# A two-stage attention and gated-convolution kernel: PSUM as eight shared banks, the whole convolution on VectorE, w_in loaded in four parts, q loaded first, and a new written order

## The chip, the core and the metric

The kernel runs on one core of one Trainium2 chip. A core has a matrix engine (TensorE, "PE" in the profile, with its weight loads "PEld" shown apart), a vector engine (VectorE, "DVE"), a scalar engine (ScalarE, "ACT"), GpSimd ("POOL") and a queue engine (SyncE, "SP"). Each engine takes its own instructions in order; semaphores order them between engines. Matmul results go to PSUM, which has eight banks; everything else lives in SBUF, and DMA queues move data between SBUF and the chip's main memory. The metric is the device time of one execution in microseconds, lower being better.

## What is computed

There are 8 batches, 8 heads, 576 positions and a head width of 64. The first stage is an attention without softmax, whose rows are normalised; the second is a gated feed-forward block with a three-tap convolution along the sequence. Inputs and output are float32.

```python
kv  = einsum('bhsd,bhse->bhde', k, v)
out = einsum('bhsd,bhde->bhse', q, kv)
rms = sqrt(mean(out * out, axis=-1, keepdims=True) + 1e-06)
x   = (out / rms * g_norm)             # then (B, S, H * D) = (8, 576, 512)
h   = maximum(x @ w_in, 0.0)           # w_in (512, 1024)
conv_out = sum over k in 0..2 of conv_w[k] * (h shifted along the sequence by k - 1, zeros outside)
gate = 1.0 / (1.0 + exp(-conv_out))
result = h * gate @ w_out              # w_out (1024, 512)
```

## The kernel before

The program is written as some forty small operations, and a long string, ORDER, lists every call of them in the order in which they are issued. Each engine keeps that order: a loop at the end ties every instruction to the one before it on its engine. A token such as `hm.0.6@2` calls `hm(0, 6)` and gives it buffer 2 of its ring; `:1` picks the other of two engines; tokens like `unread.6@0` carry a count. So the order is fixed by hand or by a search beforehand, and there is no scheduler at run time.

**Loads.** `pre` (L207) starts the first loads: k and v of heads 0 and 1 as float32 on SP's queue, the convolution weights and the gain vector (into `cw_rows`) on ACT's queue, and the rest of batch 0 in ten pieces of two heads on POOL's queue (L230), which converts to bf16 on the way. In between, DVE clears constants and POOL makes the identity. `Lq`, `Lk`, `Lv` (L290) load the other batches, batch 1 in two halves; each of q, k and v has two buffers in SBUF, so a load waits until the batch before last has been read. `Li` (L304) loads w_in in two halves of 512 columns and `Lo` (L311) w_out in two halves, all on POOL's queue. `ca` (L317) casts the float32 pieces on DVE; `ct`, `pg`, `pc` transpose the convolution weights and prepare scaled taps; `pl` (L263) sets the selection matrix `sel` on POOL.

**Attention, for a pair of heads t of a batch b.** `kv` (L344) multiplies k and v, twelve small matmuls for each pair; `kvc` (L330 on ACT, L332 on DVE) copies the two halves into a block-diagonal `kvbd`. `qt0` and `qt` (L366) transpose q on PE, and `qc0` and `qc` copy it to `qT`. `ot` (L405, L406) forms the output in PSUM, `sq` squares it on ACT, `oc` copies it to SBUF. Batch 0 is normalised directly, pair by pair: `on` (PE, a matmul with `ones`), `nl` (ACT, reciprocal root, L440), `mu0` (DVE, L455). The other batches are normalised in groups: `ss` (PE, L469) collects sums of squares with `sel`, `ln` (ACT) takes the reciprocal root, `sl` (four DVE instructions) splits it into bf16 parts, `sp` (PE, L499) spreads them again, and `mu` (DVE, L505) multiplies. The result is x of that batch.

**Feed-forward.** `hm(b, f)` (L517) makes block f of 128 columns of h for one batch: eight matmuls of 288 columns. `re` (L526, L528) applies the ReLU out of PSUM. The convolution of two blocks j runs on DVE: `ta` (L540, L541) scales the two outer taps, `aa` (L547) and `ab` (L553) add them up; `sg` (L582) is the sigmoid on ACT and `mg` (L588) the product with h on DVE. For batch 0, blocks 0 to 3 take another way: `dg` (L558) makes twelve diagonal matrices `dgw` on ACT at the start, `cm` (L568) does the three taps as matmuls on PE, and `sg` (L579) reads the sum from PSUM. Batches 0, 1, 6 and 7 go through the convolution alone, 2 and 3 together and 4 and 5 together. `om(p, m, f0)` (L598) multiplies 128 rows of a pair p of batches with w_out, eight matmuls of 512 columns, for pairs 0 and 3 in two halves of four; `ea` (L330) copies the row block out on ACT into one of eight row buffers, and `st` (L609) stores it (256 KB) from SP's queue.

**PSUM.** `ring` (L158) gives three buffers of two banks (`a0` to `a2`: q transposes, `ot`, `on`, `sp`, `hm`, `cm`, fills) and two of one bank (`b0`, `b1`: `kv`, `ss`, `om`). A buffer is free when the last reader of its former tile has done.

**Fills.** `unread.n` (L402) issues n matmuls on constants whose result nobody reads; the order places ten such groups.

ACT's tables: `act_table` (L200) loads one of two sets, one for the reciprocal root and one for the sigmoid, whenever the wanted set differs from the last.

Of the kernel before, what the change touches and what calls it, by code (L numbers as in the profile page):

```python
# [51 lines left out]
FP32 = mybir.dt.float32  # L52
# [24 lines left out]
ot.2.1@0 cm.0.1@1 sq.2.1@0 oc.2.1@0 qc.2.1@0 sg.0.1 hm.1.0@2 ot.2.2@0 hm.1.1@1 re.1.0 ot.2.3@2 sq.2.2@1 oc.2.2@1
re.1.1 sq.2.3@2 kv.3.0.4@1 oc.2.3@2 mg.0.1 hm.1.3@0 ta.1.2@0 mg.0.0 Lo.0 ta.1.0@1 kvc.3.0.4.0@1 hm.1.4@1 re.1.3
qt.3.1@2 Lo.1 Lq.4.0@0 Lv.4.0@0 ta.1.1 aa.1.0 kvc.3.0.4.1 ot.2.0@0 re.1.4 ab.1.0 sq.2.0@3 ta.1.3 qc.3.1@1 oc.2.0@3
qt.3.0@1 ot.3.3@2 ss.2@0 sq.3.3@4 qc.3.0@2 ot.3.2@0 sq.3.2@5 Lk.4.0@0 oc.3.3:1@7 ot.3.0@1 oc.3.2:1@6 om.0.0.0@1  # L80
ot.3.1@2 sq.3.0@6 aa.1.1 sq.3.1@7 hm.1.7@0 ss.3 oc.3.0:1@4 Lv.5.0@1 om.0.0.4 hm.1.5@1 ln.1@0 oc.3.1@5 re.1.7
hm.1.6@2 Lk.5.0@1 re.1.5 ab.1.1 sl.1@0 sp.2.1@0,1 al.x2@1 al.x1@0 om.0.3.0@0 ea.0.0@0 re.1.6 mu.2.2 sp.3.0@2,0
mu.2.3 sg.1.1 sg.1.3 mu.3.1 sg.1.2 mu.3.0 om.0.2.0@1 unread.1@1 sp.2.0@1,0 mu.2.1 mu.2.0 om.0.3.4 ea.0.3@1 sg.1.0
qt.4.0@2 qt.4.1@0 qc.4.1:1@3 hm.2.5@1 kv.4.0.4@0 re.2.5 kvc.4.0.4.0@0 qc.4.0@0 mg.1.0 kvc.4.0.4.1 sp.3.1@2,0 mg.1.1
Lq.5.0@1 ta.1.6@1 mu.3.2 om.0.2.4 ot.4.3@1 mu.3.3 hm.2.6@2 ea.0.2@2 sq.4.3@0 oc.4.3@1 ta.1.7 re.2.6 hm.3.7@0
Lv.6.0@0 Lk.6.0@0 ta.1.4@0 aa.1.3 ta.1.5 re.3.7 ot.4.0@1 ab.1.3 hm.2.4@2 sq.4.0@1 oc.4.0@2 Lq.7.0@0 kv.5.0.4@0
ot.4.2@0 hm.3.4@1 aa.1.2 sg.1.6 sg.1.7 kvc.5.0.4.0:1@1 om.0.1.0@1 re.2.4:1 qt.5.0@2 sq.4.2@2 oc.4.2@5 re.3.4 ab.1.2
kvc.5.0.4.1:1 ot.4.1@0 sg.1.5 hm.3.5@1 sq.4.1@3 oc.4.1@4 mg.1.3 qc.5.0@4 qt.5.1@2 ta.2.4@1 ot.5.0@0 om.0.1.4 re.3.5
# [571 lines left out]
```

## Time and profile before

| | before |
|---|---|
| median of 3 runs | 192.92 us (191.09 to 193.53) |
| the profiled execution | 192.61 us |
| its span, first to last instruction | 190.8 us |
| mean granted TensorE clock | 0.980 |
| ACT table loads | 8, 1283 ns each |
| fills (L402) | 27 in the order |
| last PE work ends, about | 186.84 us |

Times inside a profile are microseconds from the start of the span. The page gives, for each engine, its busy time, its share of the span and its number of instructions. The row PEclk cuts the span into 40 slices of 4.77 us and gives the granted TensorE clock in tenths of full speed; 9 stands for 90% or more. "PEld" is the loading of weights, which overlaps matmuls. The chain of waits follows the work that ended last back from the end, one piece per line: start, length, engine, tile, line, and how many instructions. A row by stage gives the length of the stage, then busy time and number of instructions of the engines, the granted clock, and the load of the DMA engines. Durations of matmuls are modelled and include their way through the array, so the spacing of many in a row is the better measure of what one costs.

Some rows used below, in microseconds for one: ACT `re` 0.653, `sq` 0.656, `oc` 0.661, `ea` 0.597, `nl` 0.740, `sg` 0.767 for one batch and 1.254 for two, `kvc` 0.216 (one pair of heads) to 0.378 (four); DVE `mu` 0.810, a tap of `ta` 0.38, `aa`, `ab` and `mg` 0.75 for one batch and 1.35 for two, `oc` 0.752, `qc` 0.756.

Early landings, each as issue plus time to landing: q of the four head pairs of batch 0 at 6.1, 8.4, 10.6 and 12.9 us; w_in's halves at 20.3 and 27.2; k, the last of batch 2's but q, at 33.6, and q of batch 2 at 36.5.

### The profile page before, as it was taken

Reading aid. Unit: us, or ns where it says so; the run is one execution under the profiler, and the core shown is the slowest. Engines: PE = TensorE matmul, PEld = TensorE weight load, DVE = VectorE, ACT = ScalarE, POOL = GpSimd, SP = SyncE. Lnnn points to the kernel's source line nnn. Section 1 sums busy time; section 2 is a strip of 40 time slices with the busy share of each in tenths; the row PEclk is TensorE's granted clock in tenths of the full one; section 3 lists DMA queues with packets and bytes.
Section 4 is the critical chain, followed back from the end, with each engine's and each line's share of the span. In section 5 each row is a group of like instructions: output and inputs, shape, how many; then the busy total and the mean of one; then the engine's idle time right before and its main releaser. Section 6 shows DMA issues by size and latency. Waiting matters only on the chain.

```text
span 190.8 us, 4315 instructions
## 1 busy us (share of the span) xinstructions
PE 177.8 (93%) x1782; PEld 105.8 (55%) x1804; DVE 144.2 (76%) x253; ACT 155.5 (81%) x256; POOL 29.0 (15%) x52
## 2 busy tenths in 40 slices
PE   5876899999999999999999999999999999999991
PEld 1334475677654676766554775455467665544440
DVE  5734158757898999988899979999999999971000
ACT  2787678899999899999999999997589989765341
POOL 7986007004400040500000000000000000000000
PEclk9996699999999999999999999999999999999999
DMA  6999999999999989995005321000510005413675
GB/s 150 196 197 204 203 204 205 203 205 206 204 204 204 168 109 204 156 200 87 0 3 195 118 77 57 0 0 3 202 73 0 3 0 220 174 46 141 226 268 193
DMA packets 26363, 26.27 MB, mean 138 GB/s; under 512 B 1232, under 2 KB 21736, under 8 KB 26344
## 3 DMA queue, kind: packets, MB, share of 16 engines
q0 software_dynamic: 20704, 15.96, 54.5%
q1 hardware_dynamic: 5600, 10.03, 14.5%
q8 instruction: 14, 0.23, 0.4%
q14 instruction: 5, 0.04, 0.1%
q10 hardware_dynamic: 40, 0.01, 0.0%
HBM read 32.52 MB, written 9.44 MB: 220 GB/s over the span
## 4 chain that ended last, share of the span: by engine, by line
PE 85%; ACT 8%; DMA 2%; issue 1%; DVE 1%; ACTq 0%
PE h_ps L517 34%; PE om_ps L598 33%; PE qt_ps L366 4%; PE kv_ps L344 4%; PE sp_ps L499 3%; PE o_ps L406 2%; ACT dgw L558 2%; DMA cw_rows<-in_g_norm_dram 2%; PE ss_ps L469 1%; ACT sq L419 1%; ACT kvbd L330 1%; PE unread_ps L402 1%; PE o_ps L405 1%; ACT taps L579 1%; PE cp_ps L568 1%
## 5 line engine op out<-in xcount | busy, mean ns | idle before, releaser
L517 PE MATMUL h_ps<-xT,w_in_sb 128*128 128x288 bf16 x512 | 68.0, 286 | 0.7 <-ACT h L526 0.4
L598 PE MATMUL om_ps<-w_out_sb,h 128*128 128x512 bf16 x276 | 65.8, 379 | 0.9 <-issue 0.3
L517 PEld LDWEIGHTS <-w_in_sb 128*128 128x128 bf16 x512 | 49.2, 98 | 17.1 <-issue 2.4
L598 PEld LDWEIGHTS <-h 128*128 128x128 bf16 x288 | 26.9, 98 | 31.7 <-issue 3.3
L526 ACT ACTIVATE h<-h_ps 128x576 bf16<-128x576 f32 x62 | 39.1, 653 | 3.3 <-PE h_ps L517 3.1
L582 ACT ACTIVATE taps<-taps,cwn 128x576 bf16<-128x576 bf16 (+1 forms) x44 | 39.9, 944 | 0.4 <-DVE taps L553 0.2
L330 ACT ACTIVATE row<-om_ps 128x512 f32<-128x512 f32 x36 | 21.5, 597 | 16.7 <-PE om_ps L598 15.8
L588 DVE TENSOR_TENSOR h<-h,taps 128x1152 bf16<-128x1152 bf16 (+1 forms) x24 | 22.8, 953 | 5.0 <-ACT taps L582 4.9
L505 DVE SCALAR_TENSOR_TENSOR xT<-o,cw,sp_ps 128x576 bf16<-128x576 f32 x28 | 21.8, 810 | 3.0 <-PE sp_ps L499 2.9
L540 DVE TENSOR_SCALAR taps<-h,cwn 128x576 bf16<-128x576 bf16 (+1 forms) x44 | 19.0, 432 | 6.5 <-ACT h L526 6.5
L547 DVE TENSOR_TENSOR taps<-taps 128x1152 bf16<-128x1152 bf16 (+1 forms) x22 | 21.4, 974 | 0.4
L553 DVE TENSOR_TENSOR taps<-taps,h 128x1152 bf16<-128x1152 bf16 (+1 forms) x22 | 21.3, 969 | 0.2
L421 ACT ACTIVATE sq<-o_ps 128x576 bf16<-128x576 f32 x28 | 18.0, 656 | 2.1 <-PE o_ps L406 1.3
L541 DVE TENSOR_SCALAR taps<-h,cwn 128x576 bf16<-128x576 bf16 (+1 forms) x44 | 18.8, 426 | 0.0
L330 ACT ACTIVATE o<-o_ps 128x576 f32<-128x576 f32 x25 | 16.4, 661 | 0.0
L332 DVE COPY qT<-qt_ps 128x1152 bf16<-128x1152 bf16 (+1 forms) x14 | 10.6, 756 | 3.2 <-PE qt_ps L366 2.9
L366 PE MATMUL qt_ps<-ident,q_sb 96*64 96x96 bf16 x384 | 12.1, 214 | 0.9 <-ACT qT L330 0.5
L366 PEld LDWEIGHTS <-q_sb 96*64 96x64 bf16 x384 | 10.1, 115 | 4.5 <-issue 4.5
L203 ACT ACT_TABLE_LOAD x8 | 10.3, 1283 | 2.1 <-issue 2.0
L402 PE MATMUL unread_ps<-fill 128*128 128x512 bf16 x26 | 10.0, 498 | 1.7 <-DVE fill L217 1.5
L290 POOL DMA_DIRECT2D v_sb<-in_v_dram x8 | 6.0, 750 | 27.8 <-PE sp_ps L499 14.4
L344 PEld LDWEIGHTS <-k_sb 96*64 96x64 bf16 x384 | 7.5, 116 | 4.1 <-issue 3.2
(71 smaller groups left out, 123.3 us busy)
## 6 DMA issues: line engine op xcount, KB each, us to landing
out_dram<-row SPq DMA_DIRECT2D x36, 256.0 KB, 2.4
v_sb<-in_v_dram POOLq DMA_DIRECT2D x6, 576.0 KB, 11.8
k_sb<-in_k_dram POOLq DMA_DIRECT2D x6, 576.0 KB, 13.2
q_sb<-in_q_dram POOLq DMA_DIRECT2D x6, 576.0 KB, 12.8
w_in_sb<-in_moe_w_in_dram POOLq DMA_DIRECT2D x2, 512.0 KB, 11.5
w_out_sb<-in_moe_w_out_dram POOLq DMA_DIRECT2D x2, 512.0 KB, 17.0
q_sb<-in_q_dram POOLq DMA_DIRECT2D x4, 144.0 KB, 5.0
q_sb<-in_q_dram POOLq DMA_DIRECT2D x2, 288.0 KB, 7.9
```

Source lines behind the costliest of these rows:

```text
L330: nc.scalar.activation(to, fr, AX.Copy)
L366: nc.tensor.transpose(ps[i * D:(i + 1) * D, r * PS:(r + 1) * PS], qkv["q", b][:, 2 * t + i, r * D:(r + 1) * D], ident[:PS, :PS])
L505: nc.vector.scalar_tensor_tensor(x_tile(b)[:, t, :].rearrange("p (e n) -> p e n", e=2), T["o32", b, t].rearrange("p (e n) -> p e n", e=2), ...
L517: nc.tensor.matmul(ps[:, e, :HS], w_in_sb[:, t, f * P:(f + 1) * P], x[:, t, e * HS:(e + 1) * HS], start=(t == 0), stop=(t == NT - 1))
L526: nc.scalar.activation(to, fr, AX.Relu)
L540: nc.vector.tensor_scalar_mul(tap[:, 0, f % 2, :n, 8:8 + S], h[:, f], cwn[:, 0, f:f + 1])
L541: nc.vector.tensor_scalar_mul(tap[:, 1, f % 2, :n, :S], h[:, f], cwn[:, 2, f:f + 1])
L547: nc.vector.tensor_add(tap[:, 1, :, :n, :S], tap[:, 0, :, :n, 7:7 + S], tap[:, 1, :, :n, 1:1 + S])
L553: nc.vector.tensor_add(y, y, h[:, 2 * j:2 * j + 2])
L582: nc.scalar.activation(y, y, AX.Sigmoid, scale=cwn[:, 1, f:f + 1])
L588: nc.vector.tensor_mul(h, h, T["tap", c, j][:, 1, :, :n, :S])
L598: nc.tensor.matmul(T["om", p, m], h[:, f, m * P:(m + 1) * P], w_out_sb[:, f, :], start=(f == 0), stop=(f == NF - 1))
```

## The change

1. PSUM is one tile of eight banks, `bank`. `banks(n)` gives one or two of them at a place that the order names, to any operation. `ring` serves SBUF alone.
2. `dg` and `cm` are gone; the four blocks of batch 0 take the DVE way like all others. The sigmoid reading PSUM is gone with them.
3. `Li` loads w_in in four parts of 256 columns.
4. In `pre`, batch 0's pieces are issued q, k, v for each pair of heads, where they were k, v, q (the first piece is q in both); the gain vector is one DMA, read twice, issued before the convolution weights.
5. ORDER is new throughout: 718 tokens in place of 711. Fills are 42 in 15 places, where there were 27 in 10; ACT loads its tables 10 times; seven `kvc` go from ACT to DVE, both `qc0` that were on DVE go to ACT, two more `oc` go to ACT and one `re` goes to DVE. `hm` of batch 0 stands before batch 1's `kv`; `om` may use any bank, and the last `om` are half rows of pair 3.

```diff
+pre@0,0,0 Lq.1.0@1 pn ps ca.k.0 pi unread.9@0 ct@0 al.x0@0 qt0.0.0@1 ca.v.0 kv.0.0.1@2 qt0.0.1@3 kvc.0.0.1.0:1@0 pg
+kvc.0.0.1.1:1 pc Li.0 al.h0@0 qc0.0.0:1@0 ot.0.0@0 unread.3@4 kv.0.1.1@2 kvc.0.1.1.1:1 qc0.0.1:1 kvc.0.1.1.0:1
+Lk.1.0@1 Lv.1.0@1 sq.0.0@0 on.0.0@4 ot.0.1@2 nl.0.0@0 mu0.0.0 Li.3 sq.0.1@1 unread.3@6 qt0.0.2@6 qc0.0.2:1@1
...
+ot.0.3@4 unread.1@2 qt.1.0@2 mu0.0.2 sq.0.3@3 qc.1.0@2 on.0.3@0 nl.0.3@3 Lk.1.2 Lv.1.2 mu0.0.3 unread.5@6 hm.0.0@0
+hm.0.1@4 kv.1.0.2@2 Li.2 re.0.0 re.0.1 kvc.1.0.2.0@1 kvc.1.0.2.1 unread.2@6 ot.1.0@2 ot.1.1@4 ta.0.0@0 hm.0.6@0
+ta.0.1 aa.0.0 sq.1.0@4 oc.1.0@4 re.0.6 ab.0.0 sg.0.0 sg.0.1 hm.0.2@6 sq.1.1@5 hm.0.7@0 qt.1.1@2 re.0.2:1 Lq.2.0@0
+ta.0.2@1 hm.0.3@6 re.0.3 qc.1.1@3 oc.1.1@5 unread.2@2 kv.1.2.2@2 mg.0.0 ta.0.6@0 Lk.2.0@0 Lv.2.0@0 pl kvc.1.2.2.0:1
+kvc.1.2.2.1 ta.0.3 unread.1@3 ot.1.3@2 ot.1.2@4 al.x1@1 re.0.7 sq.1.3@6 al.h1@1 Lq.3.0@1 ta.0.7 aa.0.1 hm.0.4@6
+sq.1.2@7 ss.1@0 Lv.3.0@1 Lk.3.0@1 ln.0@0 oc.1.3@6 re.0.4 oc.1.2@7 Lo.0 ab.0.1 unread.6@1 qt.2.0@0 aa.0.3 hm.0.5@2
+sl.0@0 ab.0.3 qc.2.0:1@4 sp.1.0@4,6 mu.1.1 mu.1.0 unread.2@0 sp.1.1@0,6 qt.2.1@4 mu.1.2 mu.1.3 sg.0.2 sg.0.7 sg.0.3
+Lo.1 sg.0.6 hm.1.2@0 kv.2.0.4@6 qc.2.1@0 mg.0.1 Lq.4.0@0 re.1.2 kvc.2.0.4.0@0 mg.0.3 ta.0.4@1 kvc.2.0.4.1 hm.1.3@4
...
+st.3.7 ea.2.8@3 ea.3.5@6 st.3.5 st.2.8 om.3.3.4 ea.3.3@4 st.3.3 om.3.6.4 ea.3.6@2 st.3.6
...
     def ring(r, shape, dtype, name, **kw):
+        return work.tile(shape, dtype, name=name, tag=f"{r}{slots.pop(0)}", bufs=1, **kw)
+
+    def banks(n, dtype=FP32):
         s = slots.pop(0)
-        p = psum if r in "ab" else work
-        return p.tile(shape, dtype, name=name, tag=f"{r}{s}", bufs=1, **kw)
+        return bank[:, s * BANK:(s + n) * BANK].bitcast(dtype) if dtype != FP32 else bank[:, s * BANK:(s + n) * BANK]
+
+    def two(ap):
+        return ap.rearrange("p (e n) -> p e n", e=2)
...
-    dgw = consts.tile([P, NF, 3, P], BF16, name="dgw")
+    bank = psum.tile([P, 8 * BANK], FP32, name="bank")
...
+        nc.scalar.dma_start(
+            out=cw_rows[NC:].rearrange("p (i d) -> p i d", i=2),
+            in_=g_norm.unsqueeze(0).unsqueeze(0).to_broadcast([1, 2, D]))
         nc.scalar.dma_start(out=cw_rows[:NC], in_=moe_conv_w.rearrange("k (f p) -> (k f) p", p=P))
-        for i in range(2):
-            nc.scalar.dma_start(out=cw_rows[NC:, i * D:(i + 1) * D], in_=g_norm.unsqueeze(0))
...
-        for n, (x, t) in enumerate([(x, t) for t in range(NT) for x in "kvq" if t or x == "q"]):
+        for n, (x, t) in enumerate([(x, t) for t in range(NT) for x in "qkv" if t or x == "q"]):
...
-        w = D_ff // 2
+        w = D_ff // 4
...
-        ps = T["ot", b, t] = ring("a", [P, 1024], FP32, name="o_ps")
+        ps = T["ot", b, t] = banks(2)
...
-        ps = T["hm", b, f] = ring("a", [P, 2, 512], FP32, name="h_ps")
+        ps = T["hm", b, f] = two(banks(2))
...
-            T["om", p, m] = ring("b", [P, D_model], FP32, name="om_ps")
+            T["om", p, m] = banks(1)
...
-    def cm(c, f):
-        ps = T["cp", c, f] = ring("a", [P, 2, 512], FP32, name="cp_ps")
-        h = span(c)[0][:, f, 0, :]
-        for e in range(2):
-            lo = e * HS
-            for k in (1, 0, 2):
-                a, b = max(lo, 1 - k), min(lo + HS, S + 1 - k)
-                nc.tensor.matmul(
-                    ps[:, e, a - lo:b - lo], dgw[:, f, k, :], h[:, a + k - 1:b + k - 1],
-                    start=(k == 1), stop=(k == 2))
...
     def sg(c, f):
         act_table("sig")
-        if ("cp", c, f) in T:
-            if f % 2 == 0:
-                T["tap", c, f // 2] = taps[slots.pop(0)]
-            y = T["tap", c, f // 2][:, 1, f % 2, 0, :S].rearrange("p (e n) -> p e n", e=2)
-            nc.scalar.activation(y, T["cp", c, f][:, :, :HS], AX.Sigmoid)
-            return
```

More of the change, by code (lines that the diff above doesn't have):

```diff
@@ L383, in qt @@
     def qt(b, u):
-        ps = T["qtps", b, u] = ring("a", [P, 2, 1024], BF16, name="qt_ps")
+        ps = T["qtps", b, u] = two(banks(2, BF16))
         for tt in range(2):
@@ L397, in unread @@
         nfill[0] = n
-        fills(ring("a", [P, 1024], FP32, name="unread_ps"))
+        fills(banks(1))
     def fills(ps):
@@ L494, in sp @@
         for t in (2 * u, 2 * u + 1):
[L495 removed]
+            T["sp", b, t] = two(banks(2))
         for e in range(2):
```

113 lines of the change are left out of this document (48 added, 65 removed).

## The prediction, on record before the changed kernel ran

> **What bounds it now.** I read the busy rows first, then the chain of waits that ended last, then the engines stage by stage.
>
> ```profile
> PE 177.8 (93%) x1782; PEld 105.8 (55%) x1804; DVE 144.2 (76%) x253; ACT 155.5 (81%) x256; POOL 29.0 (15%) x52
> ...
> PEclk9996699999999999999999999999999999999999
> ```
>
> ```profile
> 12.50:15.90 3.40, 2.18 (x41) 1.00 1.31 202
> 15.90:19.30 3.40, 2.11 (x29) 0.50 1.26 205
> 19.30:22.70 3.40, 2.92 (x32) 0.50 1.31 202
> ```
>
> ```profile
> 80.00:100.00 20.00, 19.64 (x306) 12.13 (x308) 18.14 (x27) 19.57 (x32) 0.00 (x0) 1.00 0.52 80
> 100.00:120.00 20.00, 19.89 (x154) 12.75 (x155) 18.44 (x25) 19.63 (x30) 0.00 (x0) 1.00 0.29 107
> 120.00:140.00 20.00, 19.84 (x115) 9.88 (x116) 19.69 (x27) 16.24 (x23) 0.00 (x0) 1.00 0.18 66
> 140.00:160.00 20.00, 19.95 (x144) 14.10 (x145) 19.01 (x38) 18.00 (x29) 0.00 (x0) 1.00 0.07 27
> ```
>
> ```profile
> 105.23 2.94 PE h_ps L517 x24
> ...
> 132.48 5.29 PE om_ps L598 x24
> ...
> 180.99 5.82 PE om_ps L598 x26
> 186.84 0.60 ACT row L330
> ```
>
> The third fence (length; then busy and count of PE, PEld, DVE, ACT, POOL; clock; DMA) shows three engines full together: ACT to 120 us, PE and DVE after. The chain is PE for 85% of the span, in spacings that hardly vary: 24 h_ps matmuls in 2.94 us (0.98 per `hm`), 24 om_ps in 5.29 (0.22 each). So I sum PE's work: 64 `hm` x 0.98 = 62.7; 288 om_ps x 0.219 = 63.0; 32 q transposes x 0.285 = 9.1; 32 kv units x 0.22 = 7.0; 36 `ot`/`on` x 0.25 = 9.0; 7 `ss` x 0.36 and 14 `sp` x 0.35 = 7.4; 4 `cm` x 0.88 = 3.5; 27 fills x 0.216 = 5.8. Together 167.6. PE ends at 186.84, so 19.2 us are not work. Time minus work issued so far tells where: 12.7 us at the first `hm` (23.71), 14.6 at the first of batch 1 (38.89), 17.9 at 105, 18.3 at 150, 19.2 at the end. The start loses most; after 39 us only 4.6 are lost. From 186.84, evacuation, the last store and closing take 3.96 (span 190.8), and 1.8 lie around it (192.61; the median 192.92 is 0.3 more).
>
> **The change, part by part.** *PE's work* does not fall: `cm` goes (-3.5 us) and the fills rise from 27 to 42 (+3.2): 167.4. Only the idle time can move.
>
> *ACT's work* stays too: 12 `dgw` gone (3.8 us in the chain), 7 `kvc` moved to DVE (about -1.5), one `re` less (-0.65), two `qc0` (0.64) and two `oc` (0.66) more, and 10 table loads for 8 (+2 x 1.283): about -0.9. Four sigmoids of 0.64 read taps (0.77, one batch) instead of PSUM. *DVE* gains 8 taps x 0.38, 4 adds x 0.75 and the 7 `kvc`, and loses two `qc0` and two `oc`: +4.6 us of 144. *POOL* issues two more DMAs (some 0.76 each) and sets `sel` after batch 2's loads instead of at 10.94; it is 15% busy and `ss` first needs `sel` near 31 us: nothing on the path. The transfers run without a break to 62 us in either, at 0.72 us per 144 KB landed, so landing follows from queue order: q's four parts of batch 0 at 6.1, 7, 9.1, 11.3 (were 6.1, 8.4, 10.6, 12.9); w_in's parts at 15.9, 20.2, 21.7, 27.6 (halves 20.3, 27.2); batch 2 complete at 36.2 (36.5). Merging the gain vector's DMAs brings `cw_rows` 0.2-0.3 us sooner, behind nine cold fills (0.427 each, 1.47 to 5.31) that end as late: nothing.
>
> *Start*, walked through the queues with durations of the rows, PE at full clock. kv of heads 0 ends at 7.4 (was 7.74: its casts no longer stand behind `cw`), the first `sq` starts at 8.7 (10.53: ACT no longer does `dgw` first). Then each pair of heads goes round ot-sq-on-nl (0.4 + 0.65 + 0.4 + 0.74) with `qc0` and `kvc` between, some 2.5 us: `nl` at 9.95, 12.85, 15.95, 17.95 and the last `mu0` ends at 19.55 (before 21.46). The first `hm` starts at 19.6, not 23.71, since batch 1's kv and `ot` now follow it. I give this 1.5 us of error either way.
>
> *19.6 to 38.* Much of that lead is lost again. Two of the extra table loads stand in front of work that PE needs: the one before the first sigmoid (25.0) has `sq` and `oc` of batch 1 and `re.0.3` queued behind it, and `ot` of heads 2 and 3 waits at 29.5 for the bank and copies; the one before `ln` ends at 32.35, then `sl` (1.6 us on DVE) at 34.5, `qc.2.0` holds sp's bank to 35.5, and the four `mu` end at 38.0. So batch 1's first `hm` starts at 38.05 (38.89) with 27.1 us of PE work issued (24.3): time minus work is 10.95 there, 3.65 us better.
>
> *38 to the end.* If PE loses the same 4.6 after that, it ends at 167.4 + 10.95 + 4.6 = 182.9. But ACT stands at 39.4 us exactly where it stood, 29.6 us of its own work issued (30.0), with as much left. Summed by its rows (which overlap by some 0.1 us each when queued), ACT got through 1.10 us of work per us from 39 to 128 before, 97% busy, so it cannot be pulled forward much. Sum both engines along the written order up to `sg.3.4`: ACT 116.4, PE 98.9. ACT gets there at 39.4 + (116.4 - 29.6) / 1.10 = 118.3, PE without further loss at 98.9 + 10.95 = 109.85, a gap of 8.5 us. Before, the largest such gap was 5.8 (at `oc.6.1`: 114.1 and 95.5), and PE had lost 3.5 by then, so ACT trailed PE by 2.3. The same trailing forces 6.2 of loss, 7.1 at the end: PE ends at 185.4. Were ACT's 3% of idle to vanish, the gap is 5.8, the loss 3.5 and then 0.9: 182.8. Between these ends I take the middle, 184.0, as eight banks for all tiles let PE run further ahead than three pairs and two singles, and PE's waits on its own instructions fall from 36 to none (idle of 0.2 each where the waits show them).
>
> *Tail.* The last two `om` are half rows of four matmuls, each with its own store. A store moves 256 KB at some 380 GB/s (0.7 us) and lands 2.4 after issue; fourteen stores stand in the last 10.3 us of PE's work, so the queue has drained before the last: 3.96 as before. A store behind a late one costs 0.7.
>
> Sum: 184.0 + 3.96 + 1.8 = **189.8**, taken as 189.7.
>
> **Clock.** PE's clock fell to half at 15.9 after a stretch busy 2.18 of 3.4 us in which no wait was over 0.8 us, and stayed low for 6.8. By my walk 34.5 to 38 is busy only 1.8 of 3.5, and a fall there meets dense `hm`: 3.4 us at half speed, +1.7; two such windows, +3.4. The Trainium skill (TensorE: Matmul & The Clock Gate, "HAM oscillation") says that gaps over some 3.4 us bring the clock down; by that rule no fall is due anywhere, and 189.7 stands. The trace disagrees: here a stretch 64% busy, without such a gap, was enough.
>
> **Rivals.**
> 1. *PE alone decides.* ACT's trailing is taken up by the banks: 182.9 + 5.8 = 188.7, and 186.5 if half of the 4.6 goes as well. For: PE's spacing is even and its losses small; against: ACT 97% busy.
> 2. *ACT decides, the lead is given back*: 185.4 + 5.8 = 191.2, and 192.9 with one clock fall. For: ACT's equal sum at 39.4. The Trainium skill (Trace Analysis, "Identifying the Most-Contended Engine") says to judge TensorE by weight loads, 55% here, not by matmul time; by it ACT at 81% is the bound and nothing is gained, 192. The matmuls' even spacing in the chain disagrees.
> 3. *Slower: added waits between ACT and DVE.* With all of PSUM one tile, ACT's instructions that wait for DVE rise from 29 to 47, DVE's for ACT from 60 to 75. If the 18 on ACT each stop it for the length of the DVE instruction in front, 0.4 to 0.75, that is 7 to 13 us in the stage where ACT is full: 196.9 to 202. It decides once they stop ACT for more than 0.4 each. Against: those I followed name the reader of the bank's previous tile, for which the matmul in between has waited already, so they should cost nothing; ACT's waits for taps total only 0.4 us now.
> 4. *Nothing moves*: the start is bound by landing, 192.6. Against: by queue order every load is there 1 to 5 us ahead of its use.
>
> **Chances and range.** About 2%, 3.9 us, is what a measurement of this kernel can tell from no change. The forecast with ends 188.9 to 191 has 0.43; rival 1 0.28, rival 2 (with a clock fall) and 4 0.16, rival 3 0.13. Below 189.06 lie rival 1 and a fifth of the forecast's case: faster 0.37; rival 3: slower 0.13; the rest 0.50. The range 186.5 to 194 takes in the walk's 1.5 us and a clock fall, and leaves out rival 3 and a little below.
>
> **What would show it.** The first h_ps matmul near 19.6 and batch 1's at 38; granted clock 1.0 through 14 to 24 us; PE's time minus work near 11 at 38, 16 to 17 at 120; ACT above 97% busy from 40 to 130. An ACT wait for DVE of several us in total, or PE below 19.5 busy of 20 after 45 us, would make it wrong.

## The result, and the profile after

The changed kernel took 186.57 us (median of 4 runs, 186.14 to 187.89), beside 192.29 us for the kernel before: a ratio of 0.9714, 95% interval 0.9629 to 0.9798. Ratios are taken from executions within 1.5% of the fastest of their kernel, medians from all of them. The profiled execution took 186.42 us, its span is 184.6 us. The time lies just inside the low end of the predicted range (186.5), and 3.1 us below the predicted 189.7.

The busy rows of the changed kernel and its row of granted clock, on the same page as shown for the kernel before:

```profile
PE 175.5 (95%) x1795; PEld 103.6 (56%) x1795; DVE 147.9 (80%) x269; ACT 153.5 (83%) x242; POOL 31.3 (17%) x54
...
PEclk9999999999999999999999999999999999999999
```

PE is busy for 2.3 us less, in a span 6.2 us shorter (the page of before lacks 22 of the 1804 matmuls that its weight loads count, so the true difference is larger). The dip of the clock near 16 to 23 us is gone. By stage (length; busy and count of PE, PEld, DVE, ACT, POOL; clock; DMA share; GB/s), the changed kernel:

```profile
12.50:15.90 3.40, 2.78 (x44) 1.29 (x45) 1.22 (x3) 2.51 (x6) 2.19 (x4) 1.00 1.36 198
15.90:19.30 3.40, 3.40 (x41) 2.00 (x42) 2.39 (x3) 1.69 (x3) 1.55 (x3) 1.00 1.36 195
19.30:22.70 3.40, 3.24 (x45) 1.98 (x43) 2.22 (x5) 2.21 (x5) 2.19 (x6) 1.00 1.37 201
...
80.00:100.00 20.00, 20.00 (x279) 12.45 (x278) 18.51 (x29) 19.88 (x31) 0.00 (x0) 1.00 0.40 89
100.00:120.00 20.00, 20.00 (x150) 14.27 (x148) 19.69 (x25) 19.97 (x30) 0.00 (x0) 1.00 0.17 62
120.00:140.00 20.00, 20.00 (x136) 10.09 (x134) 19.41 (x31) 17.25 (x24) 0.00 (x0) 1.00 0.25 93
```

The stretch that was busy 2.18 of 3.4 us at 12.5 is now busy 2.78, and the two behind it run at full clock. From 80 to 120 us PE, ACT and (nearly) DVE are all full. The end of the chain of waits (start, length, engine, tile, line, count):

```profile
135.14 12.85 PE bank L524 x104
...
151.67 29.37 PE bank L582 x136
181.04 0.02 issue
181.06 0.60 ACT row L337
```

104 matmuls of `hm` run without a gap, and 136 of `om`: the same costs as before, 0.99 us per `hm` and 0.22 per om_ps matmul. PE ends at 181.04 instead of 186.84, and 3.56 us follow instead of 3.96.

To see where the 6.2 us of span came from, I cut both traces at the start of the same matmuls, and set beside it PE's lag: the time minus the PE work issued by then, by the unit costs of the prediction. As in the prediction, the `hm` that starts there is counted as issued, which makes each of the first three lags 0.98 smaller than one that leaves it out; differences between the kernels are not touched by this.

| stretch | before, us | changed, us | difference | lag at its end, before | changed |
|---|---|---|---|---|---|
| start to batch 0's first `hm` | 23.71 | 18.42 | -5.30 | 12.7 | 6.6 |
| to batch 1's first `hm` | 15.18 | 18.61 | +3.43 | 14.6 | 9.9 |
| to the first `hm` of batches 4 and 5 | 66.17 | 62.12 | -4.05 | 17.9 | 12.5 |
| to the first `hm` of batches 6 and 7 | 34.71 | 34.50 | -0.21 | | |
| to the start of the last om_ps matmul | 46.64 | 47.00 | +0.36 | 19.2 (PE's end) | 13.6 |
| to the end of the span | 4.39 | 3.99 | -0.40 | | |

The first row falls by 5.3 us. The second is longer by 3.4, of which 2.0 are PE work that now stands in it (15.3 us for 13.25); the third is shorter, and 3.3 of its 4.05 are PE work that stands there no more. In lag: 6.1 us gained by the first `hm`, 1.4 lost again by batch 1's, 0.9 gained behind that. So nearly all of the gain is made in the first 18 us, and most of it is kept.

A part of the first row may lie in the execution and not in the change. PE starts at a slow pace: a 128x512 matmul takes some 610 to 630 ns at first and 380 ns later. In the profile of before the first one at the faster pace starts at 8.98 us, in that of the changed kernel at 4.86. In a_halves below, whose start differs only in how w_in is loaded, it came near 9.7, and the first `hm` was 1.1 us later than in the changed kernel. So up to some 1.1 of the 5.3 us may be this moment.

### The profile page after: what moved, and what is told of

Read it like the earlier page. It is cut to its first block, busy times and chain, and to the rows that moved or that the text cites. A ratio compares the mean times of both kernels' runs of the same rounds, so it can differ in the third digit from the quotient of the medians.

```text
span 184.6 us, 4352 instructions
## 1 busy us (share of the span) xinstructions
PE 175.5 (95%) x1795; PEld 103.6 (56%) x1795; DVE 147.9 (80%) x269; ACT 153.5 (83%) x242; POOL 31.3 (17%) x54
## 4 chain that ended last, share of the span: by engine, by line
PE 76%; ACT 13%; DVE 5%; DMA 2%; issue 1%; ACTq 1%; DVEq 0%
PE bank L582 32%; PE bank L524 28%; PE bank L373 4%; ACT h L533 3%; ACT sq L428 3%; PE bank L351 3%; PE bank L413 3%; PE bank L506 2%; DMA cw_rows<-in_moe_conv_w_dram 2%; ACT taps L566 2%; PE bank L409 2%; ACT o L337 2%; ACT L209 1%; ACT kvbd L337 1%; PE bank L412 1%
## 5 line engine op out<-in xcount | busy, mean ns | idle before, releaser
L524 PE MATMUL bank<-xT,w_in_sb 128*128 128x288 bf16 x512 | 67.6, 286 | 0.0
L582 PE MATMUL bank<-w_out_sb,h 128*128 128x512 bf16 x288 | 66.2, 379 | 0.0
L533 ACT ACTIVATE h<-bank 128x576 bf16<-128x576 f32 x61 | 39.6, 680 | 4.3 <-PE bank L524 4.1
L337 ACT ACTIVATE row<-bank 128x512 f32<-128x512 f32 x36 | 21.4, 610 | 11.8 <-PE bank L582 11.3
L512 DVE SCALAR_TENSOR_TENSOR xT<-o,cw,bank 128x576 bf16<-128x576 f32 x28 | 21.5, 809 | 1.3 <-PE bank L506 1.2
L428 ACT ACTIVATE sq<-bank 128x576 bf16<-128x576 f32 x28 | 19.0, 691 | 0.5 <-PE bank L413 0.5
L337 ACT ACTIVATE o<-bank 128x576 f32<-128x576 f32 x27 | 18.5, 702 | 0.0
L409 PE MATMUL bank<-fill 128*128 128x512 bf16 x42 | 13.3, 430 | 1.9 <-DVE fill L224 1.5
L373 PE MATMUL bank<-ident,q_sb 96*64 96x96 bf16 x384 | 11.0, 208 | 0.4 <-DVE xT L512 0.3
L413 PE MATMUL bank<-qT,kvbd 128*128 128x512 bf16 x32 | 11.3, 380 | 0.0
## 6 DMA issues: line engine op xcount, KB each, us to landing
w_out_sb<-in_moe_w_out_dram POOLq DMA_DIRECT2D x2, 512.0 KB, 19.1
```

The costliest lines, as they stand in the source:

```text
L337: nc.scalar.activation(to, fr, AX.Copy)
L373: nc.tensor.transpose(ps[i * D:(i + 1) * D, r * PS:(r + 1) * PS], qkv["q", b][:, 2 * t + i, r * D:(r + 1) * D], ident[:PS, :PS])
L428: nc.scalar.activation(by_r(s), natural(o), AX.Square)
L512: nc.vector.scalar_tensor_tensor(x_tile(b)[:, t, :].rearrange("p (e n) -> p e n", e=2), T["o32", b, t].rearrange("p (e n) -> p e n", e=2), ...
L524: nc.tensor.matmul(ps[:, e, :HS], w_in_sb[:, t, f * P:(f + 1) * P], x[:, t, e * HS:(e + 1) * HS], start=(t == 0), stop=(t == NT - 1))
L533: nc.scalar.activation(to, fr, AX.Relu)
```

## Experiments

Twelve kernels ran, one of them the changed kernel again. For each, the last table of this section gives the ratio and the stretches of its trace. Diffs of the order show some tokens of it and what stands in their place.

### Parts of the change, done alone to the kernel before

**Shared banks alone** (b_bank). The eight banks are one tile, and every old buffer keeps its place in it; the order is untouched.

```diff
-        p = psum if r in "ab" else work
-        return p.tile(shape, dtype, name=name, tag=f"{r}{s}", bufs=1, **kw)
...
+        at, n = (2 * s, 2) if r == "a" else (6 + s, 1)
+        ap = bank[:, at * 512:(at + n) * 512]
...
+    bank = psum.tile([P, 4096], FP32, name="bank")
```

> The kernel before with one change: PSUM is one tile of eight banks, and its three pairs and two singles are fixed places in it; the order is untouched. Theory S (the gain was made in the start, by the order): no change, within 0.7 us of before, since PE's waits on itself cost 0.2 us each at most and few stand on the chain. Theory M (shared banks as such speed the middle): 1.5 to 3 us faster, PE's loss after 39 us down from 4.6 towards 3.7. The rival of added waits: ACT waits for DVE by several us in total, 4 us or more slower.

Measured: 192.47 us, ratio 1.0036 (0.9995 to 1.0078), and every stretch within 0.2 us of the kernel before. One tile for all banks costs nothing by itself, although more instructions carry waits (239 on ScalarE's queue, where there were 216), and gains nothing while the places are fixed.

**Fills for the clock alone** (b_clock). Six more fills around the second and third round of the start; `unb` is a fill that writes one of the two single banks.

```diff
-unread.1@0 on.0.1@0
+unread.2@0 on.0.1@0
-nl.0.1@1 ot.0.2@1
+nl.0.1@1 unb.3@0 ot.0.2@1
-qc0.0.3:1 on.0.2@2
+qc0.0.3:1 unb.2@1 on.0.2@2
```

> The kernel before with six more fills between 12.5 and 16 us, five of them in the two single banks, which stand free there. If the clock's fall at 15.9 was paid for on the chain: granted clock 1.0 through 14 to 24 us, the first h_ps matmul 1.5 to 2.8 us before 23.71 (the chain has 5.6 us of PE work at half clock there), and 1 to 2.5 us less at the end. If that stage is bound by ACT and by landing instead: clock up, first h_ps within 0.7 us of 23.7, time within 0.7 us of before.

Measured: 191.05 us, ratio 0.9933 (0.9903 to 0.9964). Its stages:

```profile
12.50:15.90 3.40, 3.19 (x46) 1.59 (x46) 1.27 (x2) 2.84 (x7) 2.44 (x5) 1.00 1.31 202
15.90:19.30 3.40, 2.39 (x43) 1.30 (x44) 1.85 (x3) 2.36 (x7) 2.27 (x3) 1.00 1.26 207
```

With 3.19 of 3.4 us busy the clock stays at 1.00, where it was 0.50 from 15.9. The first `hm` comes 1.64 us sooner (22.07), and every stretch behind it is as long as before: between these two profiled executions the dip was worth 1.6 us, and 1.6 us of start are 1.6 us of the end. By the ratio it is 1.3 us. The executions of the kernel before that ran beside it span 190.65 to 194.71 us and have mean clocks of 0.973 to 0.999, so not each of them paid the same for the dip; those of b_clock span 190.69 to 191.30.

**Convolution of batch 0 on VectorE alone** (b_dve). `dg` and `cm` go, and `ta`, `aa`, `ab` of blocks 0 to 3 stand where the `cm` stood.

```diff
-dg.2 ca.k.0 dg.1 ca.v.0
+ca.k.0 ca.v.0
...
-mg.0.2 cm.0.0@0 hm.1.2@1 re.0.1 sg.0.7 mg.0.3
+mg.0.2 ta.0.0@1 hm.1.2@1 re.0.1 ta.0.1 aa.0.0 ab.0.0 sg.0.7 mg.0.3
...
-cm.0.1@1 sq.2.1@0 oc.2.1@0 qc.2.1@0 sg.0.1
+sq.2.1@0 oc.2.1@0 qc.2.1@0 sg.0.1 ta.0.2@0 ta.0.3 aa.0.1 ab.0.1
```

> The kernel before with batch 0's blocks 0 to 3 convolved on DVE like the others: twelve diagonal matrices on ACT and 24 matmuls on PE are gone, taps and adds on DVE come in near where the matmuls stood. If the work counts: PE has 3.5 us less, ACT's first square starts some 1.5 to 2 us sooner (10.53 before), together 2 to 4 us faster. If DVE's 5.3 us more stand in front of the q copies of batch 2 and the sigmoids: first h_ps earlier, but PE waits at 40 to 48 us and half or more is given back, 0 to 2 us faster.

Measured: 201.04 us, ratio 1.0469 (1.0399 to 1.0540): slower, where both expectations had it faster. Three things show. First the start, by stages:

```profile
12.50:15.90 3.40, 2.22 (x45) 1.36 (x45) 0.82 (x1) 2.94 (x7) 3.27 (x9) 0.80 1.31 202
15.90:19.30 3.40, 2.66 (x46) 1.65 (x45) 1.48 (x2) 1.62 (x3) 1.86 (x3) 0.50 1.26 206
19.30:22.70 3.40, 3.34 (x23) 1.26 (x20) 0.82 (x1) 2.25 (x6) 0.19 (x1) 0.50 1.31 202
```

The first `sq` starts 1.2 us sooner (9.31), but the clock falls sooner too, and the first `hm` starts at 23.57, where it was. ScalarE's freedom alone bought nothing at the first `hm` in this order. Second, the middle, in the chain of waits:

```profile
41.87 0.77 DVE taps L552
...
42.66 0.77 ACT taps L581
43.43 0.54 ACT h L525
43.97 0.26 ACT kvbd L329
...
44.26 0.39 ACT kvbd L329
...
44.70 0.20 PE o_ps L404
```

The sigmoid of block 0 waits for the last add of its taps; `re` and batch 2's `kvc` are queued behind it on ACT, and `ot` waits for them on PE. Third, the clock falls twice more in this stretch (slices of 4.98 us):

```profile
PEclk9995599996957999999999999999999999999999
```

The trace has it at 0.50 from 45.3 to 48.7 us and from 55.5 to 62.4. The stretch from batch 1's to the first `hm` of batches 4 and 5 becomes 8.1 us longer; how much of that is the waits and how much the clock is not separated. So this part by itself, put into the old order in this way, is a loss. The changed kernel has it in a new order with shared banks, without these falls.

### Parts of the start, undone in the changed kernel

**Without the fills of the start** (a_nofill): twenty fills between the first `ot` and the first `hm` are left out (the expectation counts 21).

```diff
-unread.3@4 kv.0.1.1@2
+kv.0.1.1@2
...
-mu0.0.3 unread.5@6 hm.0.0@0
+mu0.0.3 hm.0.0@0
```

> The changed kernel without its 21 fills between 7.7 us and the first h_ps matmul (the nine at 1.5 us stay). Theory S with the clock as a part of it: the clock falls to half somewhere in 12 to 23 us, the first h_ps comes 1 to 3 us after 18.42, the end 1 to 3 us later. If the fills do nothing: clock 1.0 or a fall without price, first h_ps within 0.5 us of 18.4, time within 0.7 us of the changed kernel.

Measured: 188.79 us, ratio 0.9825 (0.9742 to 0.9909). The first `hm` is 1.1 us later and the stretch to batch 1's 2.0 longer; behind that nothing differs. The row of granted clock says 1.00 throughout the profiled execution, but PE's groups between 5.5 and 13 us (line, tiles, shape, count; busy, mean ns of one; idle before) do not. The changed kernel:

```profile
L373 PE MATMUL bank<-ident,q_sb 96*64 96x96 bf16 x36 | 1.3, 209 | 0.0
...
L413 PE MATMUL bank<-qT,kvbd 128*128 128x512 bf16 x2 | 0.8, 380 | 0.0
```

Without the fills:

```profile
L371 PE MATMUL bank<-ident,q_sb 96*64 96x96 bf16 x36 | 2.0, 281 | 0.0
...
L411 PE MATMUL bank<-qT,kvbd 128*128 128x512 bf16 x2 | 1.2, 614 | 0.0
```

The same matmul took 614 ns instead of 380, and went on so to about 24 us (the first sixteen matmuls of `hm` took 4.0 us instead of 2.15). PE had not reached full pace at all by then. The fills are not free: in the changed kernel's chain of waits they stand for 3.4 of the first 18 us, and leaving them out still made the start longer.

**k and v loaded ahead of q** (a_kvq).

```diff
-for x in "qkv" if t or x == "q"]):
+for x in "kvq" if t or x == "q"]):
```

> The changed kernel with batch 0's pieces loaded k, v, q as before. If q first matters: q of heads 2 and 3 lands 1.4 us later (8.4 for 7), its transposes stand on TensorE ahead of the first ot, so the first sq starts at 8.8 to 9.5 for 7.91, the first hm at 19 to 19.6 for 18.42, and the span is 185 to 185.8. If k and v are what the start waits for: first sq at 7.4 to 8, first hm within 0.3, span 184.4 to 184.9.

Measured: 188.75 us (186.97 to 189.95), ratio 0.9751 (0.9691 to 0.9811). In the profiled execution, which is the longest of the four, the first `sq` starts at 10.45 and the first `hm` at 21.97. PE's groups between 5.5 and 13 us:

```profile
L373 PE MATMUL bank<-ident,q_sb 96*64 96x96 bf16 x24 | 1.4, 282 | 1.1 <-DMA q_sb<-in_q_dram 1.1
L413 PE MATMUL bank<-qT,kvbd 128*128 128x512 bf16 x2 | 1.2, 614 | 0.0
```

The transposes of heads 2 and 3 wait for q's landing, 1.1 us by the row: they start at 9.12 instead of 6.62, and `ot` of heads 0 and 1 stands behind them on PE (9.75 instead of 7.45). That wait is the mechanism expected. The rest of the 3.55 us is not separated: `cw_rows` landed later too (its matmul starts at 6.79, not 6.01), and PE is at its slow pace (614 again), to 13.6 us in this execution, while the shortest of the four took 186.97. So q first spares PE a wait of some 1.1 us ahead of the first `ot`; what of it reaches the end the runs do not fix, as the intervals of the two ratios overlap.

**ScalarE's activations back** (a_dg): twelve activations whose results nobody reads.

```diff
+dg.2 dg.1 dg.0 sq.0.0@0
-sq.0.0@0
...
-mu0.0.0 Li.3
+mu0.0.0 dg.3 Li.3
```

> The changed kernel with the twelve activations that made diagonal matrices put back on ScalarE (nine ahead of the first sq, three after the first nl), their result unread: 3.5 to 4 us of ScalarE in the start. If the start's lead came from ScalarE being free of them, and is kept: first hm at 20.5 to 22 (18.42), batch 1's first hm 2 to 3 later than 37.02, span 186.6 to 187.6 (184.6). If the lead is given back behind the start: first hm as late, but batch 1's first hm within 1 us, span within 0.7.

Measured: 189.87 us, ratio 0.9860 (0.9806 to 0.9914). The first `hm` starts 3.2 us later (21.61), every stretch behind it is as in the changed kernel, and the span is 3.2 longer: as expected of a start that is kept. Not all of the 3.2 us is ScalarE's queue. The first `sq` is 2.4 us late (10.35) behind nine of the activations, with PE at full pace; then PE, waiting for it, is busy only 1.20 of 3.4 us, and the clock falls:

```profile
PEclk9988999999999999999999999999999999999998
```

The trace has it at 0.50 from 12.2 to 15.7 us. So the activations cost by two ways, and the 0.8 us behind the first `sq` are not divided between them.

**w_in in halves** (a_halves).

```diff
-        w = D_ff // 4
+        w = D_ff // 2
...
-mu0.0.0 Li.3 sq.0.1@1
+mu0.0.0 Li.1 sq.0.1@1
```

> The changed kernel with w_in loaded in two halves (the first where part 0 was issued, the second where part 3 was). Span of the changed kernel 184.6, its first hm at 18.42, batch 1's first hm at 37.02. If the quarter parts matter: the first half lands some 1.5 to 2 us later than part 0 did, and the block that needs part 3 (hm.0.6, at about 22.3) starts 1 us later or more; batch 1's first hm at 37.5 to 38, span 185 to 185.6. If every part lands well ahead of its use: all times within 0.2 us, span 184.4 to 184.9.

Measured: 187.65 us, ratio 0.9725 (0.9693 to 0.9757). The span is 1.1 us longer, as in the first case expected, but not for its reason: the first `sq`, ahead of any use of w_in, is already 0.8 late (`ot` took 0.66 us instead of 0.42, PE at its slow pace until 9.7 us), and the stretch from the first `hm` to batch 1's is 18.61 in both. No block waited for a part of w_in, and the time is that of the changed kernel in a_same below (187.59). No gain of the four parts shows here.

### What holds the stretch from 18 to 38 us

**No table loads there** (a_late): a third tap buffer, and the first two sigmoids moved behind the group normalisation, beside the next four.

```diff
-ab.0.0 sg.0.0 sg.0.1 hm.0.2@6
+ab.0.0 hm.0.2@6
-mg.0.0 ta.0.6@0
+ta.0.6@2
-mu.1.3 sg.0.2 sg.0.7
+mu.1.3 sg.0.0 sg.0.1 sg.0.2 sg.0.7
```

> The changed kernel with a third tap buffer, and the first two sigmoids and their product moved behind the first group normalisation, beside the next four sigmoids: two table loads (2.57 us) and two sigmoids leave ScalarE between 25 and 38 us; 8 table loads in all. If ScalarE holds the stretch 20 to 38: batch 1's first hm 1 to 2.5 us earlier than 37.02, the end as much, span 182.3 to 183.8 (184.6). If VectorE (14.56 of 16 us busy there) holds it: batch 1's first hm within 0.5, span 184.2 to 184.9. If the sigmoids come too late for what follows: span over 185.

Measured: 186.78 us, ratio 0.9699 (0.9645 to 0.9753), not to be told from the changed kernel. ACT's busy time from 24 to 40 us fell from 15.84 to 12.68, and batch 1's first `hm` still comes 18.67 us behind the first (18.61). Its chain of waits:

```profile
14.84 12.21 DMA v_sb<-in_v_dram
27.05 0.04 issue
27.10 0.58 PE bank L350 x24
...
30.54 0.76 DVE taps L559
31.30 0.67 DVE taps L553
31.97 0.23 DVE hi L491
```

Here batch 1's v lands at 27.05 with `kv` waiting for it, and then DVE does two adds of batch 0's convolution before `sl` (L491). In the changed kernel the chain led through a table load (L209) and ACT's queue behind it:

```profile
24.11 1.12 ACT L209
...
28.78 0.66 ACT h L533
...
31.77 0.67 DVE taps L554
32.44 0.24 DVE hi L492
```

The ReLU ahead of the adds starts 10.4 us behind the first `hm` in both (28.78 here, 28.32 in a_late), and `sl` 14.0 and 14.1. Table loads, a landing and DVE's queue are level in this stretch; taking one away shows the next. The stretch behind it became 0.54 us longer (62.66), as much as the first `hm` had come sooner.

**DVE's adds moved as well** (a_late2): with the third tap buffer, `aa.0.3` and `ab.0.3` behind batch 1's `mu`, and the two sigmoids to about 49 us.

```diff
-ab.0.1 unread.6@1 qt.2.0@0 aa.0.3 hm.0.5@2 sl.0@0 ab.0.3 qc.2.0:1@4
+ab.0.1 unread.6@1 qt.2.0@0 hm.0.5@2 sl.0@0 qc.2.0:1@4
-mu.1.3 sg.0.2 sg.0.7 sg.0.3
+mu.1.3 aa.0.3 ab.0.3 sg.0.2 sg.0.3 sg.0.7
-qc.3.0@2 sg.1.3
+qc.3.0@2 sg.1.3 sg.0.0 sg.0.1
-mg.1.1 mg.0.2
+mg.1.1 mg.0.0 mg.0.2
-ta.1.2@0
+ta.1.2@2
```

> The changed kernel with a third tap buffer; the first two sigmoids and their product moved to about 47 us, and the last taps' two adds of batch 0's blocks 6 and 7 moved behind the mu of batch 1, so that sl starts when ln has ended. If VectorE's adds ahead of sl are what held batch 1 once the table loads were gone: batch 1's first hm 0.5 to 1 us nearer to the first hm than 18.61, the last om within 0.3 of 143.6 behind it, span 183.6 to 184.3 with a start as in the first profile. If the landing of batch 1's v holds it: 18.4 to 18.7, span 184.5 to 185.

Measured: 190.83 us, ratio 0.9869 (0.9830 to 0.9907): slower than the changed kernel. The stretch to batch 1's first `hm` is 18.45, the landing's case. The loss is behind it, where 62.1 us became 67.3:

```profile
49.39 1.43 ACT taps L566 x2
50.82 0.28 ACT kvbd L337
51.09 0.02 issue
51.11 0.44 DVE kvbd L339
51.55 0.02 issue
51.57 1.44 DVE h L572 x2
53.01 0.05 issue
53.06 3.32 PE bank L582 x8
```

The postponed sigmoids hold batch 3's `kvc` on ACT and the product that the first `om` reads; PE waits, and its clock was 0.76 and 0.74 in the next two stretches of 3.4 us. Moving this work later, as it was done here, did not pay.

### Which engine decides behind 38 us

**The changed kernel once more** (a_same).

> The changed kernel once more, unedited, as the measure for its neighbours and for how much its start varies: span 184.3 to 186.1, batch 1's first hm 18.6 us behind batch 0's and the last om 143.6 behind that. If the start's variation is the moment at which TensorE's rows reach full pace: the first hm moves by up to 1 us with the duration of the early ot (0.42 or 0.66), and nothing behind it changes.

Measured: 187.59 us (186.44 to 189.15), ratio 0.9740 (0.9657 to 0.9823). The profiled span is again 184.6, and the stretches behind the first `hm` agree with the first profile to the hundredth.

**More ScalarE** (a_act), four squares of batch 5 done twice:

```diff
+        if b == 5:
+            nc.scalar.activation(by_r(s), natural(o), AX.Square)
```

> The changed kernel with batch 5's four squares done twice: 2.2 us more of ScalarE near 70 to 82 us, nothing else. If ScalarE decides there (it trails TensorE by 2.3 us at the worst place): the last om 1.5 to 2.3 us later against batch 1's first hm than 143.6, TensorE below 19.5 busy of 20 between 60 and 120. If TensorE alone decides: under 0.5 us, as the shared banks let it run ahead.

**More TensorE** (a_pe), eleven fills in the same place:

```diff
-hm.2.4@0
+hm.2.4+3@0
...
-hm.2.1@6
+hm.2.1+2@6
```

> The changed kernel with eleven more fills among the hm of batches 2 and 3: 2.4 us more of TensorE near 70 to 80 us, nothing else. If TensorE alone decides: the last om 2.4 us later against batch 1's first hm than 143.6. If ScalarE decides there: under 1 us, since TensorE waits for it anyway. Both this and the doubled squares at over 1.5 each would mean that the two are level.

Measured: 189.04 us for the first, ratio 0.9799 (0.9705 to 0.9892), and 188.57 for the second, 0.9800 (0.9733 to 0.9866). Neither interval is clear of that of a_same, so the reading rests on the traces, where the stretches repeat to some 0.02 us. Only the one that holds the edit moved: 62.12 became 64.81 with the doubled squares and 64.30 with TensorE's 2.4 us. The four repeats start 0.69 to 0.80 us behind the square that they repeat, where queued activations otherwise start 0.53 apart, so they took some 2.9 us of ScalarE's time and not the 2.2 expected. The stages around the edit, with more ScalarE:

```profile
74.00:78.00 4.00, 3.35 (x20) 1.71 (x19) 3.96 (x7) 3.94 (x8) 0.00 (x0) 1.00 1.31 202
78.00:82.00 4.00, 3.10 (x51) 1.90 (x51) 2.86 (x3) 3.94 (x8) 0.00 (x0) 1.00 1.32 203
```

and with more TensorE:

```profile
74.00:78.00 4.00, 4.00 (x29) 2.50 (x27) 3.96 (x7) 2.98 (x6) 0.00 (x0) 1.00 1.31 200
78.00:82.00 4.00, 3.95 (x57) 2.21 (x55) 2.34 (x3) 3.97 (x7) 0.00 (x0) 1.00 1.37 199
```

In the first, PE (the first number after the length) falls to 3.35 and 3.10 of 4 while ACT stays full; in the second, ACT falls to 2.98 while PE stays full. Each engine's extra work went to the end almost whole (2.7 of 2.9, 2.2 of 2.4): the two are level in this stage.

### All runs

`sq` and `hm` are the starts of the first ones; then the stretches from the first `hm` to batch 1's, to batches 4 and 5's, and from there to the last om_ps matmul, in us. The rows of the changed kernel and a_same, one and the same kernel, show how far a ratio moves by itself; of the other edits to the changed kernel only a_late2 has an interval clear of both, so for the rest the stretches say more.

| kernel | ratio to before | `sq` | `hm` | to batch 1 | to 4 and 5 | to the last |
|---|---|---|---|---|---|---|
| before | 1 | 10.53 | 23.71 | 15.18 | 66.17 | 81.35 |
| b_bank | 1.0036 | 10.35 | 23.52 | 15.18 | 66.11 | 81.36 |
| b_clock | 0.9933 | 10.50 | 22.07 | 15.18 | 66.18 | 81.35 |
| b_dve | 1.0469 | 9.31 | 23.57 | 15.73 | 74.23 | 81.35 |
| changed | 0.9714 | 7.91 | 18.42 | 18.61 | 62.12 | 81.50 |
| a_same | 0.9740 | 8.13 | 18.39 | 18.61 | 62.12 | 81.50 |
| a_nofill | 0.9825 | 8.77 | 19.55 | 20.64 | 62.10 | 81.50 |
| a_kvq | 0.9751 | 10.45 | 21.97 | 18.62 | 62.09 | 81.50 |
| a_dg | 0.9860 | 10.35 | 21.61 | 18.61 | 62.10 | 81.50 |
| a_halves | 0.9725 | 8.70 | 19.56 | 18.61 | 62.10 | 81.50 |
| a_late | 0.9699 | 7.60 | 17.88 | 18.67 | 62.66 | 81.50 |
| a_late2 | 0.9869 | 7.75 | 18.03 | 18.45 | 67.31 | 81.50 |
| a_act | 0.9799 | 8.10 | 18.36 | 18.60 | 64.81 | 81.50 |
| a_pe | 0.9800 | 8.15 | 18.43 | 18.61 | 64.30 | 81.50 |

## Why the prediction was right or wrong

Its time was 3.1 us too long against the median and 3.3 against the profiled execution, and 0.07 us less would have fallen below the range. In the profile the sum was too high by about 1.05 at batch 1's first `hm`, by 1.95 more behind it, and by 0.4 at the tail: three terms were mis-sized. The change came out as clearly faster, to which the prediction gave 0.37, and not as one that can't be told from no change, to which it gave 0.50.

- **The start** was walked rightly. Predicted: first `sq` 8.7, last `mu0` ending at 19.55, first `hm` at 19.6, with 1.5 us of error. Measured: 7.9, 19.1 and 18.4 (`mu` of the last pair ends behind the first `hm`'s start, since the block's first matmuls read the earlier pairs). The walk took 19.6 behind the last `mu0`; 0.8 of the 1.2 is the first `sq`. That ScalarE's twelve activations mattered is shown (a_dg, 2.4 us at the first `sq`, 3.2 at the first `hm` with the fall of the clock that they brought), q first in kind (a_kvq, a wait of 1.1 us), and the clock (b_clock, 1.6 us). These are not parts of a sum: each was tried alone, and they overlap. b_dve shows what the walk assumed in passing: "PE at full clock" is a condition; where the clock fell, freeing ScalarE gave nothing at the first `hm`. How near the walk came is partly luck: with PE at its slow pace to 9.7 us, a_halves has its first `hm` at 19.56, the walk's own number.
- **"Much of that lead is lost again"** held in size and not in cause. The lag rose from 6.6 to 9.9, so 1.4 us of the lead went. The prediction laid it to two table loads, which do stand on the chain of waits; but a_late took both away and gained nothing, because the landing of batch 1's v and DVE's adds ahead of `sl` end as late.
- **The failed step is "Between these ends I take the middle, 184.0".** The frame of it was right: ACT trails PE by 2.3 us at `sg.3.4` (it starts at 113.66, PE's work puts it at 98.9 + 12.5 = 111.4), just as the prediction carried over from before, and a_act and a_pe show that in the same stretch, near 78 us, a little more of either engine's work moves the end. The rate was wrong. ACT got through 86.8 us of its own work, counted with the row lengths of before, between 39.0 and 114.9: 1.14 per us instead of 1.10; at 1.10 it would have needed 3.0 us more. That is the end of the bracket at which "ACT's 3% of idle" vanishes, and the whole of it vanished. PE ended at 181.04, below even that end (182.8): 1.05 us because it came to batch 1 sooner, and 0.7 because it lost 3.7 us from there on, not the 4.4 of that end. ACT's groups from 39 to 113.7 us (busy, mean ns of one; idle before and what ended it), in the kernel before:

```profile
L526 ACT ACTIVATE h<-h_ps 128x576 bf16<-128x576 f32 x30 | 19.4, 656 | 0.4 <-PE h_ps L517 0.2
...
L421 ACT ACTIVATE sq<-o_ps 128x576 bf16<-128x576 f32 x22 | 14.3, 657 | 0.7 <-PE qt_ps L366 0.4 <-PE o_ps L406 0.2
```

and in the changed one:

```profile
L533 ACT ACTIVATE h<-bank 128x576 bf16<-128x576 f32 x35 | 22.9, 694 | 0.1
...
L428 ACT ACTIVATE sq<-bank 128x576 bf16<-128x576 f32 x22 | 15.1, 696 | 0.0
```

  ACT used to wait for PE's products; now they are there. (That a row of ScalarE reads longer in the changed kernel, 694 ns for 656, is no added cost: see the last section.) The prediction credited the eight banks. b_bank shows that banks alone do nothing; it is the new order, with them or by itself: the new order on fixed pairs of banks was not tried, so their shares stay open.
- **The tail** was 3.56, not 3.96, and not because of the stores: from the issue of the last store to the end of its last packet both kernels take 1.7 us. The 0.4 us lies behind that. At the end SP waits for the semaphores of all queues one after another, some 0.06 us apart. In before the last store's semaphore comes second in that list, so that seven more waits follow it; in the changed kernel it comes last, when the others have been passed. The prediction took the tail over as it was and had no term for this list.
- **The merged gain DMAs** were to bring `cw_rows` 0.2 to 0.3 us sooner, to no effect. The first matmul that reads it starts at 6.01, later than the 5.49 of before, and the changed kernel's chain of waits begins with this landing:

```profile
1.98 3.90 DMA cw_rows<-in_moe_conv_w_dram
6.01 0.21 PE bank L249
```

  PE stood idle for 0.7 us there, and the DVE work on the taps that follows from it stands on the chain up to 9.1 us. The issue of the merged load took ACT's queue 1.19 us, and the convolution weights are issued behind it, at 1.98; before, they were issued first, at 0.75. So "nothing" was wrong; what an earlier landing would be worth was not tried.
- **The clock**: no fall came in the profiled execution. The stretch from 34.5 to 37.9 was busy 2.62 of 3.4, not 1.8. The trace of before, where a stretch 64% busy without a long gap brought the clock down, has its like in b_dve (2.22 of 3.4 us busy, clock 0.80 in it and 0.50 in the next two).
- **The signs named beforehand.** The granted clock of 1.0 from 14 to 24 us came, and ACT was busy for over 99% from 40 to 130, with no wait for DVE between 38 and 114. PE's lag was 9.9 at batch 1's first `hm` (near 11 expected) and 12.4 at 118, where 16 to 17 was expected at 120: here, too, the loss behind 39 us was put too high.
- **Slips in the working.** The terms given for ACT's own work add up to -0.8 us, and to -0.3 with the four sigmoids, not to -0.9; the sum of the time does not use it.
- **Rivals.** The first gave the time (186.5) by the wrong mechanism: PE alone does not decide, since ScalarE's extra work cost 2.7 us. The second had ScalarE deciding, which holds beside PE, and the lead given back, which does not: in a_dg, a_kvq, a_halves and b_clock every microsecond of the start arrives at the end of the profiled execution. The Trainium skill's page Perfetto Trace Analysis ("Identifying the Most-Contended Engine"), by which TensorE's headroom is judged by weight loads (and by the arithmetic done) and not by matmul time, read as in the prediction would have had nothing gained and extra TensorE work free. These traces disagree: weight loads are at 56%, and a_pe's 2.4 us of fills cost 2.2. The third, added waits, fell with b_bank, and in the changed kernel ACT's waits for DVE come to 2.4 us in all, each of them behind 140 us. The fourth, the start bound by landing, fell with the first row of the table of stretches, though the landing of `cw_rows` begins the chain, and in a_late that of batch 1's v came to stand on it.

## What to carry to other kernels

A microsecond of the start was a microsecond of the end here, because the written order behind it runs in the same lengths whenever it begins: cut the traces at the same instruction, and compare stretch by stretch, before asking which engine is the fullest. When two engines look full, give each a little more work in the same place: both moved the end here, so neither rate alone could give the forecast, and ScalarE's 3% of idle was worth some 3 us. Whoever takes work off the start should see what keeps PE dense there afterwards.

## What the runs showed of the hardware

The row of granted clock does not show PE's slow pace before its first rise: in the profiled execution without the fills it says 1.00 from the beginning, while a 512-column matmul took 614 ns instead of 380 to about 24 us. The durations of matmuls show it, the clock row doesn't. The record behind the row does: its first entry stands at 24.04 us in that trace, at 4.93 in the changed kernel's and at 9.06 in that of before, each where the durations change, and the row counts the time ahead of it as 1.00. The three other executions of a_nofill, 0.7 to 1.2 us shorter, show a mean of 0.962, so the mean clock does not even rank them. Moreover, the moment of the rise differs between executions whose first 5 us hold the same nine fills: by the durations it comes near 4.9 us in the changed kernel's profile, 9.7 in a_halves and 13.6 in a_kvq. Between the first two the first `hm` moved by 1.1 us. The Trainium skill (TensorE: Matmul & The Clock Gate, "What's actually happening") says that the window is free-running, so that the number of slow matmuls varies from run to run; these traces agree. Queued activations of 576 columns on ScalarE start every 0.53 us where their rows say 0.65 to 0.73, and the row grows with the queue while the spacing stays: in one unbroken run of the changed kernel from 0.65 us at 65.40 to 0.73 at 69.65. So rows sum to more than the time, and a longer row need not be a slower instruction. Counted with the row lengths of before, 1.14 us of rows per us is what a full ScalarE gave here, and 1.10 already meant idle time.
